# A dense weight loaded in two halves, and a new order of the pieces, in a kernel of memory-augmented attention beside a SiLU layer

## The chip, the cores and the metric

The kernel runs on one core of one Trainium2 chip. The metric is the device time of one execution in microseconds, as a median of several runs. The core has five engines that work beside each other, each through its own list of instructions in order: TensorE (PE in the profile, with its weight loads as PEld), VectorE (DVE), ScalarE (ACT), GpSimd (POOL) and SyncE (SP), which here only issues transfers. ScalarE issues a few transfers too.

## What is computed

`x` is normalised by rows (layer norm), and the result is fed to two branches whose outputs are added to `x`: an attention of 32 heads of 16 columns over 2048 tokens, cut into four segments of 512 with a memory carried from segment to segment, and a dense layer pair with SiLU. Cut to what matters:

```python
def _A_ref(x, wq, wk, wv, wo, beta):          # x: 1 x 2048 x 512, H = 32, Dh = 16, N = 4 segments of L = 512
    ...
    for s in range(N):
        logits = jnp.einsum('bhqd,bhkd->bhqk', qs, ks) * scale + mask      # causal inside a segment
        a_dot = jnp.einsum('bhqk,bhkd->bhqd', _softmax(logits, axis=-1), vs)
        num = jnp.einsum('bhld,bhde->bhle', phi(qs), M)
        den = jnp.einsum('bhld,bhd->bhl', phi(qs), z)[..., None] + 1e-06
        outs.append(g * (num / den) + (1.0 - g) * a_dot)
        M = M + jnp.einsum('bhld,bhle->bhde', phi(ks), vs)
        z = z + jnp.einsum('bhld->bhd', phi(ks))
    ...
    return o @ wo

def _B_ref(x, w1, w2):                        # w1: 512 x 1792, w2: 1792 x 512
    return _silu(x @ w1) @ w2

xn = _layernorm(x)
return x + _A_ref(xn, A_wq, A_wk, A_wv, A_wo, A_beta) + _B_ref(xn, B_w1, B_w2)
```

`phi(t)` is `t + 1` above zero and `exp(t)` below.

## The kernel before, in words

All work is cut into some 1,100 pieces, each a short function, and the string `ORDER` at the top lists them by name. A loop at the end of the kernel walks the string, looks each name up in `PIECES` and calls it; nothing is rescheduled afterwards. So the order in the string is the order of the instructions on each engine, and an engine whose next instruction waits holds up all that it has behind it. Waits are on counters: one for each compute engine, and eight that the transfers of SyncE and ScalarE use in turn, so that a transfer may also wait for the one that used its counter before.

A name is letters and numbers with dots. In the list that follows `s` is the segment, `dt` a block of 128 columns (eight heads), `ft` one of 14 blocks of 128 of the 1792 dense columns, `j` one of four blocks of 128 tokens, `t` one of 16 such blocks in all.

- `xs t`, `xq`/`xi t`, `xg t.n`: row statistics on VectorE, and the reciprocal root, on ScalarE and VectorE for the first four blocks and on GpSimd (lines 275 and 278) for four blocks at once after that. `Nv t` normalises on VectorE (line 293). `X`/`Xv`/`Xa` transpose on TensorE and copy; `XD t` transposes by a transfer on SyncE (line 726) into `xnT`.
- `k`, `q` `s.dt.part`, `h s.ft.part`: half of a projection, four products of 256 columns in segment 0 (line 325) and two of 512 after it (line 314). `v s.j.part`: two of 512. `kv`, `qv`, `vv` copy out on VectorE, `ka`, `qa`, `va` on ScalarE (lines 340, 350, 357); with every copy of k GpSimd makes a second one, `kTo`, that keeps odd heads only (line 341).
- `S t`: one of 80 score batches, `t = 20 s + 5 dt + b`. TensorE fills the one score tile `psS` (four of the eight banks, line 642), ScalarE takes the exponential of 128 x 2048 scores (line 649), GpSimd clears the masked corner in one or two instructions (line 657). Batches with `b` of 0 and 3 have one instruction of 512 columns, 2 one of 1024, 1 and 4 two of 512.
- `E n`, `O n`: products of the weights with v for even and odd heads (line 676), each of five batches' exponentials. `Ev`/`Ea`, `Ov`/`Oa` copy out (lines 699 and 706) and move rows by transfers on SyncE: two for an even copy, six for an odd one (lines 691 and 710).
- `ha s.ft`, `hv s.ft`: SiLU, a tanh on ScalarE (line 438) and a product on VectorE (line 443). `fp`/`gp`, `fa`/`ga`, `fv`/`gv`: phi of k and of q on GpSimd, ScalarE and VectorE (lines 368, 374, 384). `tanh` is one small operation on beta.
- `t`, `m`, `mv`, `mw`: the memory's update. `s`, `sv`, `r`, `w` (and `R`, `W` in the last segment): denominators and their reciprocals. `d`/`dv` and `z`/`zv`: two transfers each that spread them over rows (line 523, four buffers) and a product on VectorE (lines 545, 535). `n`/`nv`: the memory's part of the output (lines 549, 556).
- `o s.j.i`: one product of the output, `i` below 14 with `w2`, above with `wo` (line 595). `oh i.half` is half of such a product for the last block of tokens. `xl s.j` loads a block of x again (line 562), `st s.j` and `sh half` add it and store (lines 569, 574; 613, 617).
- `lw i`: a load of a weight on ScalarE's queue (line 176). The other weights are loaded from SyncE at the very start.

`psS` is one tile, so a score batch waits for the exponential before it. All other results on TensorE share four banks, each taken again when the copy that empties it is done.

The lines that the prediction follows most are these:

```python
psS = psatt.tile([P, 4, L], F32, name="psS")          # psatt has one buffer
exp = nc.scalar.activation(out=Pb[:, :, :], in_=psS[:, :, :], func=AF.Exp, scale=SCALE)
...
def load_w(eng, w_sb, W, k0, k1):
    eng.dma_start(out=w_sb[:, k0:k1, :], in_=W.rearrange("(ko ki) n -> ki ko n", ki=P)[:, k0:k1, :])
```

Of the kernel before, what the change touches and what calls it, by code (L numbers as in the profile page):

```python
# [16 lines left out]
ones0 ones1 zeros xs0 xs1 xq0 xi0 busy44 xq1 Nv0 xi1 X0.1 Nv1 Xa0.1 busy6 X1.1 Xa1.1 v0.0.0 xs2 xs3 xq2 v0.0.1 xq3 xi2 va0.0 v0.1.0 Nv2 v0.1.1 va0.1 xi3 X2.1 Nv3 odd tb Xv2.1 k0.0.0 X3.1 Xv3.1 q0.0.0 q0.0.1 qv0.0 k0.0.1 xs7 xs4 ka0.0 k0.2.0 xs6 fp0.0  # L17
S0 v0.3.0 k0.1.0 k0.2.1 fa0.0 xs5 xg4.4 v0.3.1 kv0.2
S2 q0.1.0 k0.1.1 q0.1.1 vv0.3 fp0.2 v0.2.0 kv0.1 fa0.2 Nv7 Nv4
S1 qv0.1 v0.2.1 h0.10.0 h0.10.1 h0.7.0 xs8 vv0.2 ha0.10 h0.7.1 hv0.10 ha0.7  # L20
S4 Nv5 h0.4.0 h0.4.1 ha0.4 h0.11.0 hv0.7 k0.3.0 h0.11.1 ha0.11 xs9 hv0.11 fv0.2
S7 k0.3.1 q0.3.0 XD4 q0.3.1 hv0.4 q0.2.0 XD5 XD7 q0.2.1 fa0.1
S6 qv0.3 qv0.2 h0.13.0 h0.13.1 t0.2 v1.3.0 ha0.13 v1.1.0
S3 v1.1.1 kv0.3 Nv6 xs11 h0.5.0 hv0.13 h0.5.1 xs10 ha0.5 xg8.4 XD6 E0 vv1.1
S5 v1.3.1 lw0 hv0.5 vv1.3 k1.0.0 xs14 k1.2.0 k1.2.1
S9 h0.1.0 Ev0 Nv10 kv1.2 Nv9 h0.1.1 k1.0.1 E1 ha0.1
S13 kv1.0 h1.11.0 XD10 h0.2.0 h0.2.1 ha0.2 h1.11.1 Ev1 fv0.0 hv0.1
S8 hv0.2 tanh O0 h0.8.0 h0.8.1 bmask Ov0 q1.1.0 ha0.8 hv0.8
# [12 lines left out]
S20 r0.3 h1.10.1 k2.1.0 o0.0.3 ha1.10 hv1.0 k2.1.1 r0.1 q2.3.0
S23 r0.2 o0.0.7 gate kv2.1 q2.3.1 r0.0 xg12.4 xl0.0 h1.4.0 h1.4.1 w0 o0.0.13 hv1.10 qv2.3 ha1.4 o0.0.12
S28 z0.3 o0.1.12 o0.1.0 hv1.4 z0.0 z0.2 o0.0.4 E4 lw1 O4
S27 o0.1.11 Ev4 Ov4 k2.0.0 o0.1.2 h1.5.0 h1.5.1 o0.0.11 ha1.5 Nv12 z0.1
S25 o0.0.9 o0.0.8 o0.1.1 zv0.3 k2.0.1 hv1.5 zv0.0 fv1.2 q2.1.0 XD12 ga1.3 fp1.3 o0.0.1 kv2.0 o0.0.5
S29 o0.1.8 o0.1.6 fa1.3 o0.0.14 q2.1.1 h1.1.0 zv0.2 o0.1.9 o0.1.17 qv2.1
S26 o0.2.0 o0.0.17 h1.1.1 o0.1.14 o0.1.7 fv1.3 xl0.1 o0.2.7 gp1.3 zv0.1 ha1.1 t1.0 hv1.1 o0.1.16 o0.1.13
S30 o0.0.15 o0.0.16 st0.0 o0.1.15 o0.2.14 t1.3 ga1.1 o0.2.8 o0.1.10 E5 Nv14
S31 gv1.3 o0.2.1 Ev5 h1.3.0 fp1.1 fa1.1 o0.2.4 o0.1.4 o0.2.3 Nv15 O5 mw0.0
S32 o0.1.3 XD14 o0.1.5 h1.3.1 o0.2.10 o0.2.17 o0.2.9 o0.2.12 mw0.2 xl0.3 ha1.3 st0.1 o0.2.6  # L50
S33 Ov5 o0.2.16 o0.2.5 t1.2 o0.2.11 fv1.1 ga1.0 k2.3.0 v2.0.0 Nv13 gp1.0 hv1.3 k2.3.1
S38 v2.0.1 o0.2.15 kv2.3 h1.6.0 h1.6.1 o0.2.2 ha1.6 XD15 vv2.0 o0.2.13
S34 gv1.0 o0.3.3 hv1.6 h1.13.0 h1.13.1 v2.3.0 st0.2 q2.2.0 ha1.13
S37 ga1.2 t1.1 q2.2.1 o0.3.16 o0.3.6 gp1.2 hv1.13 o0.3.2 qv2.2 o0.3.5 E6
S36 v2.3.1 Ev6 o0.3.7 vv2.3 h1.12.0 o0.3.1 gv1.1 h1.12.1 ha1.12 o0.3.12
S35 hv1.12 fa2.0 fp2.1 XD13 O6 q2.0.0 q2.0.1 gv1.2 h1.2.0
S39 Ov6 q3.3.0 xl1.1 q3.3.1 h1.2.1 qv2.0 E7 ha1.2 qv3.3 Ev7
S40 k3.1.0 hv1.2 k3.1.1 o0.3.0 o0.3.9 O7 ga2.2 Ov7 kv3.1
S47 fp2.0 o0.3.4 m1.2 q3.1.0 q3.1.1 mv1.2 qv3.1 s1 sv1
S41 r1.0 m1.0 v3.3.0 o0.3.11 o0.3.8 xl1.0 fv2.0 mv1.0 v3.3.1 va3.3 o0.3.17 r1.3 fp2.2  # L60
S44 o0.3.15 h2.3.0 q3.0.0 fa2.1 q3.0.1 v3.1.0
S42 r1.2 r1.1 v3.1.1 qv3.0 h2.3.1 o0.3.13 w1 o0.3.14 d1.1 z1.1 vv3.1 o0.3.10 ha2.3 fv2.1 v3.0.0 hv2.3
S43 t2.0 st0.3 v3.0.1 h2.4.0 h2.4.1 z1.2 E8 vv3.0 ha2.4
S45 hv2.4 h1.7.0 h1.7.1 dv1.1 k3.2.0 k3.2.1 o1.0.0 fa2.2 o1.0.5 ha1.7
# [37 lines left out]
def kernel(  # L102
# [13 lines left out]
    nc = tc.nc  # L116
# [4 lines left out]
    DT = D // P  # L121
# [7 lines left out]
    FT = F // P  # L129
# [28 lines left out]
    w2_sb = cpool.tile([P, FT, D], BF16, name="w2_sb")  # L158
# [16 lines left out]
    def load_w(eng, w_sb, W, k0, k1):  # L175
        eng.dma_start(out=w_sb[:, k0:k1, :], in_=W.rearrange("(ko ki) n -> ki ko n", ki=P)[:, k0:k1, :])  # L176
# [618 lines left out]
```

## Time and profile before

| | us |
|---|---|
| median of three runs | 231.92 (231.20 to 232.23) |
| the profiled execution, its whole time | 231.23 |
| its span in the profile | 229.50 |
| TensorE busy with products | 221.5 (97%) |
| ScalarE busy | 198.9 (87%) |
| VectorE busy | 171.8 (75%) |
| GpSimd busy | 114.8 (50%) |
| 80 exponentials, line 649 | 150.2, 1.88 each |
| first and last exponential start | 12.86 and 206.06 |

The granted clock of TensorE is full in every slice of the span. Products are pipelined: the mean of one that the profile lists (0.38 us for 512 columns) is longer than the distance at which they follow each other (0.216 us), so a busy TensorE is not yet one at its peak. In a timeline row the columns are start and duration in microseconds, engine, line, operation, output and inputs, shapes and count; in brackets stands the idle time of the engine before it, with what ended it. In the chain of waits the run is followed back from its end, at each step to what released it.

Where the time of the middle goes, by stretches of the span (all us):

| stretch | TensorE | VectorE | ScalarE | GpSimd |
|---|---|---|---|---|
| 0 to 10 | 8.17 | 6.08 | 5.40 | 3.49 |
| 20 to 30 | 9.87 | 9.14 | 9.99 | 5.33 |
| 90 to 100 | 10.00 | 7.32 | 9.96 | 6.25 |
| 180 to 200 | 19.98 | 16.01 | 18.56 | 9.02 |
| 215 to 229.5 | 11.00 | 7.98 | 0.00 | 0.00 |

### The profile page before, as it was taken

The page shows a single profiled execution, that of the slowest core. Times are in us where ns is not written, and L with a number is a line of the kernel's source. Part 1 is how long each engine was busy: PE and PEld are TensorE (multiplying, and loading weights), DVE is VectorE, ACT ScalarE, POOL GpSimd, SP SyncE. Part 2 cuts the span into 40 slices and gives each one's busy share as a digit, 9 for nine tenths or more (in the row PEclk, how much of TensorE's full clock was granted, in tenths as well). Part 3 has the DMA queues.
Part 4 walks back from the last instruction along what each step waited for, and adds up shares of the span by engine and source line. Part 5 has one row for each costly group of instructions (what it writes and reads, how often), then busy time and mean ns, then how long its engine had stood idle before and what let it go on. Part 6 is the DMA issues. An engine that isn't in the chain of part 4 may idle for free.

```text
span 229.5 us, 5243 instructions
## 1 busy us (share of the span) xinstructions
PE 221.5 (97%) x1984; PEld 103.6 (45%) x1984; DVE 171.8 (75%) x349; ACT 198.9 (87%) x179; POOL 114.8 (50%) x173
## 2 busy tenths in 40 slices
PE   7899999989999999999999999999999999999993
PEld 7657645445533433333433433344433443434552
DVE  4699997978978758866596967845796868874744
ACT  3789999999999999999999999999999999996000
POOL 6068557576474586564574474655444473332000
PEclk9999999999999999999999999999999999999999
DMA  6993256014302424241115232203032111132132
GB/s 200 366 371 70 57 169 195 18 31 74 73 17 54 140 72 101 59 94 30 33 38 98 75 83 76 64 9 98 25 96 81 52 32 58 32 88 83 34 116 94
DMA packets 34778, 20.40 MB, mean 89 GB/s; under 512 B 15680, under 2 KB 34240, under 8 KB 34752
## 3 DMA queue, kind: packets, MB, share of 16 engines
q1 hardware_dynamic: 32128, 17.45, 27.6%
q10 hardware_dynamic: 2624, 2.62, 3.7%
q8 instruction: 15, 0.25, 0.5%
q14 instruction: 11, 0.09, 0.1%
HBM read 9.96 MB, written 2.10 MB: 53 GB/s over the span
## 4 chain that ended last, share of the span: by engine, by line
PE 77%; ACT 13%; DMA 3%; issue 2%; DVE 1%; SPq 1%; DVEq 0%; ACTq 0%
PE ps L314 26%; PE psO L595 25%; PE psS L642 10%; ACT Pb L649 10%; PE psV L676 8%; DMA wq_sb<-in_A_wq_dram 3%; PE psS L595 3%; PE ps L325 3%; ACT th L438 2%; PE ps L549 1%; ACT ex L374 1%; PE psM L400 1%; SPq L176 1%; DVE hT L443 1%; DVE o_out L569 1%
## 5 line engine op out<-in xcount | busy, mean ns | idle before, releaser
L649 ACT ACTIVATE Pb<-psS 128x2048 bf16<-128x2048 f32 x80 | 150.2, 1878 | 5.2 <-PE psS L642 4.0
L657 POOL TENSOR_SCALAR_AFFINE_SELECT Pb<-Pb 128x512 bf16<-128x512 bf16 (+1 forms) x112 | 81.2, 739 | 82.2 <-ACT Pb L649 81.8
L595 PE MATMUL psO<-w_sb,hT 128*128 128x512 bf16 x196 | 60.2, 381 | 0.0
L443 DVE SCALAR_TENSOR_TENSOR hT<-th,ps 128x512 bf16<-128x512 bf16 x56 | 37.8, 681 | 21.1 <-ACT th L438 20.9
L314 PE MATMUL ps<-xnT,w_sb 128*128 128x512 bf16 x168 | 45.5, 380 | 0.0
L595 PEld LDWEIGHTS <-hT 128*128 128x128 bf16 x238 | 22.0, 98 | 26.7 <-issue 6.6
L438 ACT ACTIVATE th<-ps 128x512 bf16<-128x512 f32 x56 | 32.6, 595 | 0.4 <-PE ps L314 0.4
L314 PEld LDWEIGHTS <-w_sb 128*128 128x128 bf16 x168 | 15.2, 98 | 18.0 <-issue 3.1
L676 PE MATMUL psV<-Pb,Vz 128*32 128x128 bf16 (+3 forms) x512 | 22.2, 301 | 0.0
L642 PE MATMUL psS<-qT,kT 16*128 16x256 bf16 (+3 forms) x256 | 17.3, 301 | 1.3 <-ACT Pb L649 0.3
L595 PE MATMUL psO<-wo_sb,oT 128*128 128x512 bf16 x56 | 18.2, 380 | 0.0
L314 PE MATMUL ps<-wv_sb,xnT 128*128 128x512 bf16 x64 | 18.0, 381 | 0.1
L642 PE MATMUL psS<-qT,kTo 32*128 32x384 bf16 (+3 forms) x256 | 17.2, 299 | 0.8 <-ACT Pb L649 0.2
L676 PEld LDWEIGHTS <-Vz 128*32 128x32 bf16 x512 | 11.0, 96 | 13.4 <-issue 5.5
L341 POOL TENSOR_SCALAR kTo<-kT,pm_odd 128x512 bf16<-128x512 bf16 x16 | 11.9, 745 | 10.2 <-ACT kT L340 8.2
L325 PE MATMUL ps<-xnT,w_sb 128*128 128x256 bf16 x112 | 14.6, 273 | 0.0
L706 DVE CAST odd<-psV 128x512 bf16<-128x512 f32 x15 | 10.3, 686 | 4.9 <-PE psV L676 4.8
L314 PE MATMUL ps<-xnT,wk_sb 128*128 128x512 bf16 x48 | 13.3, 380 | 0.1
L350 DVE CAST qT<-ps 128x512 bf16<-128x512 f32 x16 | 10.8, 680 | 3.5 <-PE ps L314 2.2
L642 PEld LDWEIGHTS <-kT 16*128 16x128 bf16 x256 | 5.8, 91 | 16.7 <-issue 15.5
L314 PE MATMUL ps<-xnT,wq_sb 128*128 128x512 bf16 x48 | 12.8, 380 | 0.0
L325 PEld LDWEIGHTS <-w_sb 128*128 128x128 bf16 x112 | 10.4, 98 | 3.9 <-issue 1.5
(95 smaller groups left out, 258.0 us busy)
## 6 DMA issues: line engine op xcount, KB each, us to landing
spr<-rz SPq DMA_DIRECT2D x56, 64.0 KB
x_res<-in_A_x_dram SPq DMA_DIRECT2D x16, 128.0 KB
out_dram<-o_out SPq DMA_DIRECT2D x15, 128.0 KB
w_sb<-in_B_w_dram SPq DMA_DIRECT2D x1, 1792.0 KB
w_sb<-in_B_w_dram ACTq DMA_DIRECT2D x1, 1792.0 KB
x_hi<-in_A_x_dram SPq DMA_DIRECT2D x2, 512.0 KB
oraw<-odd SPq DMA_DIRECT2D x64, 16.0 KB
wv_sb<-in_A_wv_dram SPq DMA_DIRECT2D x2, 256.0 KB
```

The lines of the kernel that those rows point to most:

```text
L314: nc.tensor.matmul(sts[s][key][:, :], lhsT=lhsT(ki), rhs=rhs(ki), start=(ki == 0), stop=(ki == DT - 1))
L325: nc.tensor.matmul(sts[s][name, i][:, cols], lhsT=w_sb[:, ki, i * P : (i + 1) * P], rhs=xnT[:, ki, cols], start=(ki == 0), stop=(ki == DT ...
L341: nc.gpsimd.tensor_scalar(out=kTo[:, dt, :], in0=kT[:, dt, :], scalar1=pm_odd[:, 0:1], scalar2=1.0, op0=ALU.mult, op1=ALU.mult,)
L350: copy(out=seg_tile(s, "qT")[:, dt, :], in_=sts[s].pop(("q", dt))[:, :])
L438: nc.scalar.activation(out=th[:], in_=sts[s]["h", ft][:, :], func=AF.Tanh, scale=0.5)
L443: nc.vector.scalar_tensor_tensor(out=st["hT"][:, ft, :], in0=st.pop(("th", ft))[:], scalar=1.0, in1=st.pop(("h", ft))[:, :], op0=ALU.add, ...
L595: mm = nc.tensor.matmul(st["psO", *key], lhsT=lhsT, rhs=rhs, start=len(done) == 1, stop=len(done) == FT + DT)
L642: nc.tensor.matmul(psS[:, g, c0 : c0 + nq], lhsT=kk[rows, dt, kt * P : (kt + 1) * P], rhs=st["qT"][rows, dt, kt * P : L], start=True, stop ...
L649: exp = nc.scalar.activation(out=Pb[:, :, :], in_=psS[:, :, :], func=AF.Exp, scale=SCALE)
L657: mask = nc.gpsimd.affine_select(out=blocks, in_=blocks, compare_op=ALU.is_ge, fill=0.0, base=0, pattern=[[0, blocks.shape[1]], [1, P]], c ...
L676: nc.tensor.matmul(psV[32 * g : 32 * g + 32, kt * P : L], lhsT=Vzs[s % 2][:, kt, 4 * dt + g, par : par + 2, :].rearrange("p a d -> p (a d) ...
L706: copy(out=odd[:], in_=sts[s].pop(("psV", 1))[:, :])
```

## The change

`w2` (14 blocks of rows) was loaded by one transfer, `lw0`, of 1792 KB behind S5; now `lw0` loads its first seven blocks behind S7 and `lw1` the other seven behind S14. `wo`, which was `lw1` behind S28, is now `lw2` behind S26. And the whole string `ORDER` is a new one: the same pieces in another order, with other choices of the engine for a few copies (`qa0.0`, `ka0.2`, `va3.2` and `Oa14` on ScalarE where they were on VectorE; `va3.3`, `ka3.0` and `Ea9` the other way). No function is changed.

The diff, cut to the start, the loads and the end. The string's last line, very long, is wrapped here:

```diff
@@ ORDER
-... Xv2.1 k0.0.0 X3.1 Xv3.1 q0.0.0 q0.0.1 qv0.0 k0.0.1 xs7 xs4 ka0.0 k0.2.0 xs6 fp0.0
-S0 v0.3.0 k0.1.0 k0.2.1 fa0.0 xs5 xg4.4 v0.3.1 kv0.2
-S2 q0.1.0 k0.1.1 q0.1.1 vv0.3 fp0.2 v0.2.0 kv0.1 fa0.2 Nv7 Nv4
-S1 qv0.1 v0.2.1 h0.10.0 h0.10.1 h0.7.0 xs8 vv0.2 ha0.10 h0.7.1 hv0.10 ha0.7
...
-S5 v1.3.1 lw0 hv0.5 vv1.3 k1.0.0 xs14 k1.2.0 k1.2.1
...
-S28 z0.3 o0.1.12 o0.1.0 hv1.4 z0.0 z0.2 o0.0.4 E4 lw1 O4
...
-S79 w3 h3.13.0 h3.13.1 ha3.13 hv3.11 o2.1.15 xl2.1 o2.1.1 h3.6.0 h3.10.0 hv3.13 d3.3 o2.1.0
-S78 o2.1.14 h3.10.1 R0.3 h3.9.0 h3.6.1 R0.1 o2.1.13 d3.0 o2.1.11 R0.0 o2.1.6 R0.2 W0 ha3.10
-S76 o2.1.9 hv3.10 ha3.6 o2.1.3 d3.1 o2.1.8 h3.9.1 o3.1.0 o3.1.2 dv3.0 o3.1.13 ha3.9 dv3.3
...
- st3.2 o3.1.10 oh13.0 o3.0.17 o3.1.15 o3.1.17 o3.1.3 sh0 oh16.1 oh9.1 st3.0 oh4.1 st3.1 oh1.1 oh15.1 oh0.1 oh17.1 oh7.1 sh1
+... Xv2.1 k0.0.0 X3.1 Xv3.1 xs4 k0.2.0 xs5 k0.0.1 q0.0.0 ka0.0 xs7 q0.0.1 k0.2.1 k0.3.0 xs6 qa0.0 xg4.4 ka0.2
+S2 q0.1.0 v0.3.0 k0.1.0 k0.3.1 kv0.3 fa0.2 fp0.2
+S3 q0.1.1 qv0.1 fa0.0 v0.3.1 Nv6 k0.1.1 h0.7.0
+S1 Nv7 v0.2.0 Nv5 v0.2.1 Nv4 XD6 h0.7.1 ha0.7 vv0.3 kv0.1 h0.11.0 vv0.2 xs10
+S4 hv0.7 XD5 xs9 XD4 h0.11.1 q0.2.0 h0.4.0 XD7 h0.4.1 ha0.11
+S8 xs11 ha0.4 v1.1.0 v1.1.1 hv0.11 q0.2.1 vv1.1 xs8 h0.13.0
+S0 qv0.2 h0.10.0 hv0.4 h0.10.1 h0.13.1 ha0.10 h0.2.0 fp0.0 ha0.13 q1.1.0 xg8.4
+S7 q1.1.1 h0.2.1 fv0.2 hv0.10 hv0.13 E0 O0 lw0
+S9 qv1.1 fp0.3 Ev0 h0.5.0 xs12 ha0.2 Nv10 v1.3.0 h0.5.1 Ov0 t0.2 v1.3.1
...
+S14 kv1.0 v1.0.1 qv0.3 q1.0.0 q1.0.1 lw1 E1 qv1.0
...
+S26 r0.0 q2.3.1 k2.0.0 lw2 hv1.10 k2.0.1 o0.0.9 qv2.3 v2.2.0
...
+S75 h3.2.0 h3.2.1 o2.2.3 hv3.8 O14 Oa14 s3 ha3.2
+S78 o2.2.5 sv3 h3.11.0 xl2.1 r3.3 h3.11.1 st2.2 r3.1 h3.7.0 o2.1.17 r3.0 h3.7.1 o2.1.3 ha3.11 hv3.2 r3.2
+S76 o2.1.2 w3 o2.1.0 o2.1.4 hv3.11 o2.1.13 h3.9.0 d3.3 ha3.7 h3.9.1 o2.1.16 ha3.9 o2.1.7 R0.3 d3.2 o2.1.14
+S79 R0.0 d3.1 R0.1 R0.2 hv3.7 o2.1.9 h3.6.0 W0 o2.1.11 h3.6.1 o2.1.10 h3.10.0 ha3.6 o2.1.12 h3.10.1 hv3.9 ha3.10 o2.1.8 hv3.6
+S77 d3.0 o3.0.12 hv3.10 o3.0.9 dv3.3 o3.0.2 h3.13.0 h3.13.1 o2.1.6 ha3.13 o2.1.15 z3.0 dv3.2 o2.1.5 hv3.13
+ oh12.0 o3.0.8 o3.2.3 oh6.0 o3.0.11 oh5.0 o3.0.0 dv3.0 o2.1.1 z3.2 st2.1 E15 O15 o3.1.3 xl3.1
...
+ oh5.1 xl3.2 oh17.1 o3.1.17 xl3.3 o3.0.17 o3.2.15 o3.2.17 o3.2.9 o3.1.8 oh11.0 oh10.0 oh13.1 o3.1.15 oh2.1 oh15.1
+ oh1.1 oh14.1 st3.0 o3.1.1 oh17.0 st3.2 sh1 o3.1.9 o3.1.12 sh0 st3.1
@@ PIECES
-        "lw": lambda i: load_w(nc.scalar, *((w2_sb, B_w2, 0, FT), (wo_sb, A_wo, 0, DT))[i]),
+        "lw": lambda i: load_w(nc.scalar, *((w2_sb, B_w2, 0, FT // 2), (w2_sb, B_w2, FT // 2, FT), (wo_sb, A_wo, 0, DT))[i]),
```

## The prediction

> **What bounds the kernel now.** I read the page first, then ScalarE's timeline between the exponentials, then the two ends of the run on all engines, and last the waits of SyncE's queue.
>
> ```profile
> PE 221.5 (97%) x1984; PEld 103.6 (45%) x1984; DVE 171.8 (75%) x349; ACT 198.9 (87%) x179; POOL 114.8 (50%) x173
> PE 77%; ACT 13%; DMA 3%; issue 2%; DVE 1%; SPq 1%; DVEq 0%; ACTq 0%
> ```
>
> TensorE looks like the limit, with ScalarE behind it. The timeline of ScalarE says how the two are tied:
>
> ```profile
> 30.27 1.88 ACT L649 ACTIVATE Pb<-psS 128x2048 bf16<-128x2048 f32 x1
> 30.28 0.39 ACTq L176 DMA_DIRECT2D w_sb<-in_B_w_dram  x1
> 32.65 1.88 ACT L649 ACTIVATE Pb<-psS 128x2048 bf16<-128x2048 f32 x1 [0.50 <-PE psS L642]
> 34.42 0.59 ACT L438 ACTIVATE th<-ps 128x512 bf16<-128x512 f32 x1
> 35.05 1.88 ACT L649 ACTIVATE Pb<-psS 128x2048 bf16<-128x2048 f32 x1
> ...
> 198.06 1.88 ACT L649 ACTIVATE Pb<-psS 128x2048 bf16<-128x2048 f32 x1 [0.18 <-PE psS L642]
> 199.84 1.08 ACT L438 ACTIVATE th<-ps 128x512 bf16<-128x512 f32 x2
> 200.79 1.90 ACT L649 ACTIVATE Pb<-psS 128x2048 bf16<-128x2048 f32 x1
> ```
>
> Exponentials start 2.38 us apart whether one small ScalarE operation stands between them (32.65 to 35.05) or none (30.27 to 32.65): there is one score tile psS, so an exponential must end, the next scores be written and the next exponential start. The beat is 2.375 us (the usual gap in this timeline). It is lengthened by two things only: two small operations in one gap (198.06 to 200.79; the six such gaps average 2.753, so +0.378 each), or more than 2.375 us of TensorE pieces between two score batches. So the run is three parts: the first exponential starts at 12.86; 79 gaps take 193.20 (last start 206.06) of which 79 x 2.375 = 187.63 is the beat and 5.57 is excess; the tail from there to the span's end at 229.50 is 23.44.
>
> **The change part by part.** The arithmetic is the same; each part is costed against these three.
>
> *The load.* One issue of 0.39 us on ScalarE's queue becomes two, and wo's issue moves. All three stand in gaps that hold no small operation (behind S7, S14, S26); the row at 30.28 shows such an issue under an exponential and the gap still 2.38. Cost 0; without that cover, 0.39 each. The two halves start at about 27.8 and 37.7 (beats counted from 12.86). w2 is first read by o0.0.7, near 64: over twenty microseconds of other work hide the second half. In the built program the second issue waits for the completion of a row move of O0, since the eight completion counters go round; that move is issued near 33, five microseconds earlier. On SyncE the sixth transfer of O0's copy waits for the first half, which has had about 7 us by then; behind it stand only t0.2 and XD10, whose readers are many beats away. Cost 0.
>
> *The start.* wq is awaited until 10.25 with TensorE idle 0.65 now; the new list puts k0.2.0 and k0.0.1 there. But S2 needs qa0.0 too and ScalarE also takes ka0.2 before the exponential. From rows: k0.0.1 ends 10.56, q0.0.1 11.43 (0.109 us a 256-wide product), qa0.0 runs 11.65 to 12.24, scores at 12.4, exponential at 12.85. Gain 0.0.
>
> *GpSimd before S8.* The rstd pair xg4.4 now stands ahead of kT's odd copy ka0.2, of S2's mask and of everything up to kv0.1, whose odd copy the fifth batch S8 reads.
>
> ```profile
> 12.46 0.70 POOL L341 TENSOR_SCALAR kTo<-kT,pm_odd 128x512 bf16<-128x512 bf16 x1 [8.18 <-ACT kT L340]
> ...
> 15.81 1.03 POOL L278 TENSOR_TENSOR rstd_all<-rstd_all,expo 128x4 f32<-128x4 f32 x1
> ...
> 16.92 1.03 DVE L293 TENSOR_SCALAR xn_t<-x_hi,mv_all,rstd_all 128x512 bf16<-128x512 bf16 x2
> 16.94 0.86 POOL L341 TENSOR_SCALAR kTo<-kT,pm_odd 128x512 bf16<-128x512 bf16 x1
> ```
>
> xg4.4 waits for four row statistics, which start when x's second load has landed: after wq's 10.25 in the same queue and before 11.95, where the first one ran without waiting for it. Taking 11.75 and the 3.28 us the four took, they end at 15.03, xg4.4 at 16.34 (0.20 + 1.03 and a gap). Then 0.86 (odd copy), 1.12 (mask), 0.70, 0.63, 0.64, 1.23, 0.70 from the GpSimd groups: 22.2, while S8 could be written at 12.86 + 3 x 2.375 + 1.88 + 0.06 = 21.9. Cost 0.3. Bounds: 0 if the data lands at 10.25; 1.5 if three odd copies take the longest of the trace (1.01), with the longest mask (1.42) and pos (0.78).
>
> The row to see is the last: beside two normalisations the odd copy took 0.86 instead of 0.70, and they 1.03 instead of 2 x 0.41. The Trainium skill (GPSIMD Engine Reference, Specifications) says that GpSimd shares its SBUF interface with VectorE, contending when VectorE runs in a 2-port mode or has two SBUF inputs; Trainium Architecture — The Big Picture (What this means for kernel authors) calls it an exclusive lock. The trace agrees that both stretch. It speaks against this change, for all four normalisations now fall beside the GpSimd chain; a full lock of 4 x 0.41 us would be an estimated 1.6 instead of the 0.16 taken here.
>
> *The gaps.* Gaps with two small operations go from six to nine (S0, S5, S11, S62, S66, S60, S75, S76, S79), gaps with none from four to seven, which gives nothing back. Eight at 0.378 are 3.02. In the ninth, S79, TensorE is longer still: four halves of h (8 products), five o, at 0.216 each (four L314 products in 0.86 in the chain of waits), 0.21 for the scores and 2 x 0.10 for the changes of tile shape: 3.22, excess 0.84. S71 and S74 have 2.57 and 2.47: 0.29. In S75, ScalarE's first operation is the copy Oa14, which waits for O14: 0.15. With S8's 0.3 that is 4.60. The same bookkeeping gives 3.85 for before, whose gaps show 5.57: 1.72 is small waits it does not name (S18, S30, S44, S61, S75 and dust). I charge the new list the same 1.72; nothing in VectorE's or SyncE's work per gap says otherwise. Bounds 0.5 and 3.0. Excess 6.32, or 0.75 more; the last exponential starts at 206.81.
>
> *The tail on TensorE.* Behind the last scores stand 66 products of 512 columns instead of 67, and 36 of 256 in both: -0.2. Now the last product is issued at 225.73 and ends 225.84, 19.78 after the last exponential; that becomes 19.57: 226.38.
>
> *The last stores.*
>
> ```profile
> 223.98 0.69 DVE L569 SCALAR_TENSOR_TENSOR o_out<-psS,x_res 128x512 bf16<-128x512 f32 x1 [1.79 <-PE psS L595]
> 224.59 0.41 DVE L613 SCALAR_TENSOR_TENSOR o_half<-psS,x_res 128x256 bf16<-128x256 f32 x1
> 224.92 1.28 DVE L569 SCALAR_TENSOR_TENSOR o_out<-psO,x_res 128x512 bf16<-128x512 f32 x2
> 226.11 0.41 DVE L613 SCALAR_TENSOR_TENSOR o_half<-psS,x_res 128x256 bf16<-128x256 f32 x1
> ```
>
> Now st3.2 starts 0.31 after oh17.0 is issued, and 2.2 us of products remain to cover it. In the new list oh17.0 stands third from the end, 0.54 before TensorE finishes, and st3.2, sh1, sh0, st3.1 queue behind it on VectorE: 0.31 + 0.61 + 0.33 + 0.33 + 0.68 after its issue, by the row distances above. So the last store is issued at 226.38 - 0.54 + 2.26 + 0.05 = 228.15 against 227.06, and the span ends 2.44 later as now: 230.6.
>
> **Sum.** +0.75 - 0.21 + 0.55 = +1.1 on 229.50. What lies around the span is 231.23 - 229.50 = 1.73, so 232.3 beside the profiled 231.23. That execution is 0.69 under the median 231.92; on the median's scale I forecast **233.0**, 0.47% longer, at the edge of the 0.5% that a measurement of this kernel can tell from no change.
>
> **The rivals.**
>
> *GpSimd decides (slower).* If its chain before S8 takes the upper price, the beat slips 1.5 instead of 0.3: 234.2. It decides once kv0.1's odd copy ends after 21.9. For: 0.86 and 1.01 among the copies. Against: thirteen of the sixteen copies took 0.69 to 0.71.
>
> *SyncE's tail (slower).* E15 to nv3.3 runs through row moves, reciprocals and a spread: E15 starts 209.39 and nv3.3 ends 222.19 now, 12.8 us. In the new list E15 starts near 210.3, and oh17.1, the first reader, is due 3.14 us before TensorE ends, at 223.24: a margin of 0.1 to 0.2 after the same 12.8. st2.1 and xl3.1 now stand ahead of the moves (0.4), two x_res loads no longer ahead of the spread (0.45). Beyond that each microsecond counts in full; one more, like the spread waits of 2.3 and 1.1 in VectorE's list, gives 233.9.
>
> *The waits go (faster).* If the 1.72 of unnamed waits came from late SyncE transfers and the new list avoids them, and nothing else changes: 231.3; with the final stores overlapping as now, 230.7. For: in S18 the reader k2.2.0 follows two transposes (XD8, XD11) by one beat; in the new list only XD9 stands so near its reader. Against: SyncE's longest waits are for VectorE, not the reverse.
>
> *The split load holds ScalarE.* If O0's row move completes after 39, the second issue holds every exponential behind it; two microseconds late is 235. The margin above is some four.
>
> **How the numbers follow.** Forecast 0.48 (own range 232.0 to 234.0), GpSimd 0.16, SyncE's tail 0.18, waits go 0.14, held ScalarE 0.04. Slower by over 0.5% (above 233.08): all of three rivals, 0.38, less a little that is made up elsewhere, and a fifth of the forecast: 0.46. Faster (below 230.76): 0.10 of the waits' 0.14 and a little of the forecast's low end: 0.12. The rest 0.42. The range leaves a tenth out at each side: 230.9 to 234.7.
>
> **What would show it.** First exponential within 0.2 of 12.86; the fifth at 22.6 or 22.7 and not 24; nine gaps near 2.75 and that of S79 near 3.2; last exponential near 206.8; four stores on VectorE in a row at the end, the last a 512-wide one. The prediction is wrong if any gap before S62 exceeds 3 us, or if TensorE stands idle after the last scores.

## The result and the profile after

The changed kernel takes 233.31 us (median of 9 runs, 232.43 to 234.15), beside 232.05 us (230.85 to 233.07) for the kernel before on the same chip. The ratio is 1.0062, with a 95% interval of 1.0035 to 1.0090. Run once more in the study, beside 17 runs of before, it gave 1.0076 (1.0050 to 1.0102). By the ratios it is slower by 1.4 to 1.8 us. The profiled execution took 232.94 us, its span is 231.2 us, and the granted clock is 0.997.

The totals of the page first: busy time of each engine, and the chain that ended last by engine.

```profile
PE 221.9 (96%) x1984; PEld 102.8 (44%) x1984; DVE 172.7 (75%) x348; ACT 199.2 (86%) x180; POOL 114.0 (49%) x173
...
PE 75%; ACT 7%; DVE 6%; DMA 4%; issue 2%; SPq 2%; POOL 1%; DVEq 0%; ACTq 0%
```

The work is that of before. What changed is the chain: VectorE has 6% of it instead of 1%. So some waits on VectorE are now in the path. To find them, I split each trace at the exponentials. "Excess" is what a stretch of gaps takes beyond 2.375 us for each gap. The columns are two traces of each kernel; the second of each comes from the study.

| us | before | before, again | after | after, again |
|---|---|---|---|---|
| first exponential starts | 12.86 | 12.89 | 12.72 | 13.11 |
| excess of the first 18 gaps | 0.85 | 0.95 | 2.21 | 3.36 |
| excess of the next 43 | 1.46 | 1.57 | 0.25 | 0.26 |
| excess of the last 18 | 3.27 | 3.24 | 3.59 | 3.59 |
| last exponential to the end of the span | 23.46 | 23.58 | 24.81 | 24.30 |
| span | 229.52 | 229.85 | 231.22 | 232.25 |

The new order loses 1.3 to 2.5 us in the first 18 gaps, gains 1.2 to 1.3 in the middle, loses 0.3 in the last gaps and 0.7 to 1.4 in the tail. About 0.4 us of the first two figures is only a shift: the kernel before has two gaps with two small operations among its first 18 and one in the middle (S45, 2.77 us), the new list has three and none. Here are the places, all from the timeline of after. First the gaps of ScalarE with a load issue, and with two small operations:

```profile
28.08 0.39 ACTq L176 DMA_DIRECT2D w_sb<-in_B_w_dram  x1
28.18 1.90 ACT L649 ACTIVATE Pb<-psS 128x2048 bf16<-128x2048 f32 x1
30.58 1.88 ACT L649 ACTIVATE Pb<-psS 128x2048 bf16<-128x2048 f32 x1 [0.50 <-PE psS L642]
...
200.35 1.88 ACT L649 ACTIVATE Pb<-psS 128x2048 bf16<-128x2048 f32 x1
202.12 1.08 ACT L438 ACTIVATE th<-ps 128x512 bf16<-128x512 f32 x2
203.16 1.88 ACT L649 ACTIVATE Pb<-psS 128x2048 bf16<-128x2048 f32 x1
```

These behave as forecast: 2.40 us over the load's issue, 2.81 with two operations. The same timeline, at the start:

```profile
16.23 2.83 DVE L293 TENSOR_SCALAR xn_t<-x_hi,mv_all,rstd_all 128x512 bf16<-128x512 bf16 x4
16.28 0.83 POOL L341 TENSOR_SCALAR kTo<-kT,pm_odd 128x512 bf16<-128x512 bf16 x1
...
17.07 1.14 POOL L657 TENSOR_SCALAR_AFFINE_SELECT Pb<-Pb 128x1024 bf16<-128x1024 bf16 x1
...
18.98 0.67 DVE L357 CAST Vz<-ps 128x512 bf16<-128x512 f32 x1
...
19.71 0.60 PE L325 MATMUL ps<-xnT,w_sb 128*128 128x256 bf16 x4 [0.71 <-DVE Vz L357]
...
20.69 1.88 ACT L649 ACTIVATE Pb<-psS 128x2048 bf16<-128x2048 f32 x1 [0.68 <-PE psS L642]
```

Four normalisations stand in a row on VectorE and take 2.83 us, where the four of the first blocks took 0.41 each. The copy vv0.3 behind them ends at 19.65. The product h0.11.0 needs the bank that this copy empties, and S4's scores stand behind h0.11.0 on TensorE. So the exponential of S4 starts 3.04 us after that of S1. And at the end of the span:

```profile
226.03 0.69 DVE L569 SCALAR_TENSOR_TENSOR o_out<-psS,x_res 128x512 bf16<-128x512 f32 x1 [1.48 <-PE psS L595]
226.63 0.75 DVE L613 SCALAR_TENSOR_TENSOR o_half<-psS,x_res 128x256 bf16<-128x256 f32 x2
227.19 1.13 SPq L617 DMA_DIRECT2D out_dram<-o_half  x2
227.30 0.68 DVE L569 SCALAR_TENSOR_TENSOR o_out<-psO,x_res 128x512 bf16<-128x512 f32 x1
228.43 0.38 SPq L574 DMA_DIRECT2D out_dram<-o_out  x1
```

VectorE stood idle for 1.48 us before the first of four pieces that then follow each other without a gap, and the last store is issued at 228.43, 22.03 us after the last exponential (21.00 before). It is a whole block of 128 KB, and the span ends 2.79 us later; before, it was a half of 64 KB and 2.46 us. TensorE is not what differs: its last product starts 19.64 us after the last exponential, 19.67 before. From that product to the issue of the last store it is now 2.38 us instead of 1.33.

The second trace of after shows one more place. These are SyncE's transfers in it (start, and how long the issue held the queue), and then the wait view of the same queue (microseconds waited in total, times, longest):

```profile
38.72 1.27 SPq L726 DMA_TRANSPOSE xnT<-xn_t  x1
...
43.36 2.21 SPq L726 DMA_TRANSPOSE xnT<-xn_t  x1
46.64 0.37 SPq L562 DMA_DIRECT2D x_res<-in_A_x_dram  x1
...
54.74 2.10 SPq L726 DMA_TRANSPOSE xnT<-xn_t  x1
```

```profile
SPq L562 <- DMA xnT<-xn_t: 1.0, 1, 1.0
```

The transposition of tile 10 (38.72) is followed within 0.15 us by the load of w2's second half on ScalarE's queue (38.87). In the trace's landing records, the transposition lands between 46.14 and 46.57 and the half at 46.41. The load of a residual, xl0.1 (46.64), is the first user of the buffer that tile 10 held. It waits 1.0 us, with SyncE's queue behind it, after the issue at 43.36 had already held the queue for 2.21 us where most of line 726 hold it for 1.2 to 1.3. The queue is then busy without a break until the transposition of tile 9 at 54.74. The next rows are what waits for that:

```profile
58.24 0.59 PE L314 MATMUL ps<-xnT,wk_sb 128*128 128x512 bf16 x2 [0.91 <-DMA xnT<-xn_t]
...
59.22 1.88 ACT L649 ACTIVATE Pb<-psS 128x2048 bf16<-128x2048 f32 x1 [0.88 <-PE psS L642]
```

That is k2.1.0 in S15's place, and the gap behind S15 is 3.24 us. In the first trace SyncE came to xl0.1 only at 45.20, when tile 10 had landed, and xl0.1 did not wait; the gap was 2.47, 0.1 over the beat.

### The profile page after: what moved, and what is told of

Its sections match the earlier page's. It is cut to its first block, busy times and chain, and to the rows that moved or that the text cites. A ratio compares the mean times of both kernels' runs of the same rounds, so it can differ in the third digit from the quotient of the medians.

```text
span 231.2 us, 5219 instructions
## 1 busy us (share of the span) xinstructions
PE 221.9 (96%) x1984; PEld 102.8 (44%) x1984; DVE 172.7 (75%) x348; ACT 199.2 (86%) x180; POOL 114.0 (49%) x173
## 3 DMA queue, kind: packets, MB, share of 16 engines
q10 hardware_dynamic: 2640, 2.62, 3.5%
## 4 chain that ended last, share of the span: by engine, by line
PE 75%; ACT 7%; DVE 6%; DMA 4%; issue 2%; SPq 2%; POOL 1%; DVEq 0%; ACTq 0%
PE ps L314 27%; PE psO L595 23%; PE psS L642 10%; PE psV L676 8%; ACT Pb L649 6%; DMA x_hi<-in_A_x_dram 3%; PE ps L325 3%; PE psS L595 3%; DVE stats L270 2%; ACT th L438 1%; DVE xn_t L293 1%; PE ps L549 1%; SPq L523 1%; SPq L176 1%; DVE hT L443 1%
## 5 line engine op out<-in xcount | busy, mean ns | idle before, releaser
L657 POOL TENSOR_SCALAR_AFFINE_SELECT Pb<-Pb 128x512 bf16<-128x512 bf16 (+1 forms) x112 | 80.2, 730 | 82.6 <-ACT Pb L649 81.6
L595 PE MATMUL psO<-w_sb,hT 128*128 128x512 bf16 x196 | 62.8, 381 | 0.0
L314 PE MATMUL ps<-xnT,w_sb 128*128 128x512 bf16 x168 | 46.4, 380 | 0.0
L676 PE MATMUL psV<-Pb,Vz 128*32 128x384 bf16 (+3 forms) x512 | 22.4, 301 | 0.0
L595 PE MATMUL psO<-wo_sb,oT 128*128 128x512 bf16 x56 | 19.3, 380 | 0.3 <-DVE oT L556 0.3
L642 PE MATMUL psS<-qT,kT 16*128 16x384 bf16 (+3 forms) x256 | 17.3, 301 | 0.7 <-ACT Pb L649 0.2
L325 PE MATMUL ps<-xnT,w_sb 128*128 128x256 bf16 x112 | 15.2, 273 | 1.0 <-DVE Vz L357 0.7
L706 DVE CAST odd<-psV 128x512 bf16<-128x512 f32 x14 | 9.6, 688 | 4.7 <-PE psV L676 4.5
L350 DVE CAST qT<-ps 128x512 bf16<-128x512 f32 x15 | 10.3, 685 | 3.4 <-PE ps L314 3.1
```

The costliest lines, as they stand in the source:

```text
L314: nc.tensor.matmul(sts[s][key][:, :], lhsT=lhsT(ki), rhs=rhs(ki), start=(ki == 0), stop=(ki == DT - 1))
L325: nc.tensor.matmul(sts[s][name, i][:, cols], lhsT=w_sb[:, ki, i * P : (i + 1) * P], rhs=xnT[:, ki, cols], start=(ki == 0), stop=(ki == DT ...
L350: copy(out=seg_tile(s, "qT")[:, dt, :], in_=sts[s].pop(("q", dt))[:, :])
L595: mm = nc.tensor.matmul(st["psO", *key], lhsT=lhsT, rhs=rhs, start=len(done) == 1, stop=len(done) == FT + DT)
L642: nc.tensor.matmul(psS[:, g, c0 : c0 + nq], lhsT=kk[rows, dt, kt * P : (kt + 1) * P], rhs=st["qT"][rows, dt, kt * P : L], start=True, stop ...
L657: mask = nc.gpsimd.affine_select(out=blocks, in_=blocks, compare_op=ALU.is_ge, fill=0.0, base=0, pattern=[[0, blocks.shape[1]], [1, P]], c ...
```

## The experiments

Each experiment but the last is the changed kernel with one or more edits. Times are medians beside runs of before on the same chip; the changed kernel again, **a0_after**, was 233.63 us.

> The changed kernel unaltered, beside the kernel before and the three edits on one chip. Theory: the two kernels differ by the end of the span (last store issued 1.37 us later, landing 0.33 us longer) and by 0.34 us in the last exponential, so the ratio is 1.006 to 1.008 again. Rival (the difference is one chip's or one day's): a ratio within 0.998 to 1.002.

Ratio 1.0076 (1.0050 to 1.0102): the difference holds. Here the two kernels differ by less at the end than in the first pair (0.7 us instead of 1.4) and by more at the start (2.4 instead of 1.4).

**e1_start: the normalisations spread.**

```diff
-S3 q0.1.1 qv0.1 fa0.0 v0.3.1 Nv6 k0.1.1 h0.7.0
-S1 Nv7 v0.2.0 Nv5 v0.2.1 Nv4 XD6 h0.7.1 ha0.7 vv0.3 kv0.1 h0.11.0 vv0.2 xs10
-S4 hv0.7 XD5 xs9 XD4 h0.11.1 q0.2.0 h0.4.0 XD7 h0.4.1 ha0.11
+S3 q0.1.1 qv0.1 fa0.0 v0.3.1 vv0.3 Nv5 k0.1.1 h0.7.0
+S1 kv0.1 v0.2.0 v0.2.1 XD5 h0.7.1 ha0.7 vv0.2 h0.11.0 Nv6
+S4 hv0.7 XD6 Nv4 h0.11.1 q0.2.0 h0.4.0 XD4 Nv7 XD7 h0.4.1 ha0.11
...
```

> VectorE's first normalisations of segment 1 are spread, one behind each copy, instead of four in a row, and two statistics go later. Theory: the four in a row (2.83 us beside GpSimd's work) held back the copy that frees the bank of h0.11, so the gap of 3.04 us before the exponential of S4 and that of 2.55 us before S1 fall to about 2.40, and the time falls by 0.6 to 0.85 us against the changed kernel. Rival (GpSimd's chain in front of S8's scores): the scores of S4 or S8 then wait for the odd copy, the fifth exponential stays at 23.0, and the time stays. Second rival (the work on VectorE is only moved): the stall comes back within the next three gaps, time within 0.2 us.

234.07 us, ratio 1.0106 (1.0074 to 1.0138): no gain, perhaps a loss. Both gaps that the theory named fell to 2.375 us, so the cause of the stall was right. But 0.39, 0.39 and 0.35 us came back behind S4, S7 and S9: VectorE is short of time there. The second rival was right that the work is only moved, though the time rose by 0.4 us, more than its 0.2. Besides, this execution had a stall in the middle that neither trace of after had:

```profile
121.82 6.33 SPq L523 DMA_DIRECT2D spr<-rz  x8
...
127.98 0.46 DVE L535 TENSOR_TENSOR oT<-spr,oraw 128x512 bf16<-128x512 bf16 x1 [1.46 <-DMA spr<-rz]
...
129.09 1.02 PE L314 MATMUL ps<-xnT,wk_sb 128*128 128x512 bf16 x4 [0.63 <-DVE oraw L699]
...
131.14 1.88 ACT L649 ACTIVATE Pb<-psS 128x2048 bf16<-128x2048 f32 x1 [1.29 <-PE psS L642]
```

The same eight spreads in a0_after:

```profile
122.10 5.25 SPq L523 DMA_DIRECT2D spr<-rz  x8
```

One of the eight issues held SyncE for 1.68 us instead of 0.60. zv1.1 waited for its tile, the copy Ev8 behind it on VectorE was late, and k3.2.0 waited for the bank. This cost 1.3 us in two gaps.

**e2_end: another order of the last products and stores.**

```diff
-... o3.2.9 o3.1.8 oh11.0 oh10.0 oh13.1 o3.1.15 oh2.1 oh15.1 oh1.1 oh14.1 st3.0 o3.1.1 oh17.0 st3.2 sh1 o3.1.9 o3.1.12 sh0 st3.1
+... o3.2.9 st3.0 o3.1.8 o3.1.15 st3.2 o3.1.1 o3.1.9 o3.1.12 st3.1 oh11.0 oh10.0 oh17.0 sh0 oh13.1 oh2.1 oh15.1 oh1.1 oh14.1 sh1
```

> The products after the last scores are put in another order so that the four last pieces of output end one after another, the last two as halves: the stores stand on VectorE before the last half's products are issued. Theory (the end of the span is the queue of four stores): the last store is issued at about 227.1 instead of 228.4, lands 2.4 us later instead of 2.8, and the time falls by 1.0 to 1.7 us. Rival (the last products or SyncE's chain in front of them set the end): the last store follows TensorE's end, which does not move, and the time falls by less than 0.4 us.

232.63 us, 1.0 less than a0_after, at the low end of what was expected; ratio 1.0040 (1.0018 to 1.0061).

```profile
226.72 2.06 SPq L574 DMA_DIRECT2D out_dram<-o_out  x3
227.72 0.69 DVE L569 SCALAR_TENSOR_TENSOR o_out<-psO,x_res 128x512 bf16<-128x512 f32 x1 [0.39 <-PE psO L595]
228.33 0.75 DVE L613 SCALAR_TENSOR_TENSOR o_half<-psS,x_res 128x256 bf16<-128x256 f32 x2
229.20 0.81 SPq L617 DMA_DIRECT2D out_dram<-o_half  x2
```

The last exponential of this trace starts at 208.56 (the first one started late, at 14.14), so the end of the span at 232.24 is 23.68 behind it. Over all traces the distance from the last exponential to the end is 24.26 to 24.85 in seven traces with the changed kernel's end (mean 24.48), and 23.14 to 24.00 in five with this one (mean 23.54); before has 23.46 and 23.58. So the end of the order costs 0.9 to 1.0 us. Where it goes can be read from the start of TensorE's last product to the issue of the last store: 2.38 to 2.41 us in all seven, 1.35 in four of the five (0.91 in e10, which issues one store on ScalarE), 1.33 and 1.52 in the two of before. The queue of four pieces behind the last products is the cause. The size of the last store is not shown to be one: from its issue to the end of the span the seven take 2.60 to 2.86 us with a block of 128 KB, the five 2.53 to 3.07 with a half of 64 KB.

**e4_gaps: the loads issued from SyncE, small operations into the freed gaps.**

```diff
-S0 qv0.2 ... ha0.10 h0.2.0 fp0.0 ha0.13 q1.1.0 xg8.4
-S7 q1.1.1 h0.2.1 ...
+S0 qv0.2 ... ha0.10 h0.2.0 fp0.0 q1.1.0 xg8.4
+S7 ha0.13 q1.1.1 h0.2.1 ...
...
-        "lw": lambda i: load_w(nc.scalar, ...
+        "lw": lambda i: load_w(nc.sync, ...
```

> The three weight loads are issued from SyncE's queue at the same places, and of the small ScalarE operations, one of S0's two goes to S7, one of S5's two to S6 and S6's one to S14. Theory: a second small operation in a gap costs 0.38 us and a load issue takes ScalarE's gap without lengthening it, so two gaps of 2.73 to 2.77 become 2.38 and S7 and S14 stay at 2.38: the last exponential 0.75 us earlier, the time 0.6 to 0.8 us less. Rival (the small operations only wait where they stand, and the loads' issues on SyncE hold back its moves): under 0.2 us, or slower.

235.95 us, 2.3 us more: a clear miss. The gaps of S0 and S5 did shrink (to 2.62 and 2.37), but those behind S7 and S6 became 4.25 and 4.11:

```profile
31.54 0.73 PE L676 MATMUL psV<-Pb,Vz 128*32 128x512 bf16 x16 [1.56 <-DVE hT L443]
...
32.65 1.88 ACT L649 ACTIVATE Pb<-psS 128x2048 bf16<-128x2048 f32 x1 [1.88 <-PE psS L642]
```

The tanh that was moved past one exponential delays its SiLU on VectorE by a beat, the SiLU empties a bank, and O0 on TensorE wants that bank. Behind S6 it is the same: a product of v waits 1.35 us for the SiLU of the second moved tanh. A second operation in a gap costs 0.38 us; to move it to the next gap costs five times that where the four banks have no spare.

**e3_one_load: w2 in one piece at the first half's place.**

```diff
-        "lw": lambda i: load_w(nc.scalar, *((w2_sb, B_w2, 0, FT // 2), ...
+        "lw": lambda i: load_w(nc.scalar, *((w2_sb, B_w2, 0, FT), ...
-S14 kv1.0 v1.0.1 qv0.3 q1.0.0 q1.0.1 lw1 E1 qv1.0
+S14 kv1.0 v1.0.1 qv0.3 q1.0.0 q1.0.1 E1 qv1.0
```

> The changed kernel with w2 loaded in one piece at S7 (the first half's place); the second half's place in S14 stays empty. Theory (the second half's transfer holds up SyncE): the transposition of tile 10, issued 0.1 us before that load, landed 7.4 us later, at 46.1 to 46.6; the load of the residual (xl0.1) waits 1.0 us for its buffer, with SyncE's queue behind it, so the transposition of tile 9 is issued at 54.7 and the product of S15 waits 0.9 us for it. Without that load tile 10 lands within 3 us, xl0.1 does not wait, the gap of S15 falls from 3.24 to about 2.40, and the time falls by 0.6 to 0.9 us against the changed kernel. Rival (the split costs nothing, as forecast): S15's gap and the time stay within 0.3 us. Second rival (the one long transfer of about 11 us holds the moves of the first heads' sums instead): a stall before S14, time up by 0.5 us or more.

235.36 us, 1.7 us more than a0_after: the theory's forecast was wrong, the second rival right in direction, though not in the place (the gaps up to S14 were hardly longer). Tile 10's transposition landed 2.4 us after its issue, so the second half's load had indeed held it. But now the row moves of the first heads (31.06 to 33.42) landed only at 36.0 to 37.5, with the load, and SyncE waited for them:

```profile
SPq L710 <- DMA zraw<-oraw: 3.3, 1, 3.3
```

The queue was later than in a0_after (tile 9's transposition at 55.10) and the gap behind S15 3.40. In this order, one piece is worse than two by the times. The trace does not show all of it: it is of the fastest of the six executions (234.30), and its first 18 gaps have only 0.2 us more than a0_after's. In the kernel before, one piece (issued 30.28, landed by 37.99) held the row moves of E0 in the same way (issued from 33.11, landed by 38.29), but the moves of the odd heads, which come after them, were issued only at 39.07, and nobody waited. No run has the split load in the old order.

**e7_xl_late: xl0.1 behind tile 9's transposition.**

```diff
-S13 Nv9 h1.11.0 vv1.0 k1.1.0 k1.1.1 xl0.1 hv0.1 ...
+S13 Nv9 h1.11.0 vv1.0 k1.1.0 k1.1.1 hv0.1 ...
-S19 v1.2.1 hv0.9 ha0.6 kind XD9 O2 E2 vv1.2 Ev2 hv0.6
+S19 v1.2.1 hv0.9 ha0.6 kind XD9 xl0.1 O2 E2 vv1.2 Ev2 hv0.6
```

> The changed kernel with one word moved: the residual's load xl0.1 is issued on SyncE behind the transposition of tile 9 (S19) instead of ahead of that of tile 11 (S13). Both halves of w2 stay. Theory (xl0.1 waits on SyncE for the buffer that tile 10's late transposition holds): the transposition of tile 9 is issued about 1.0 us earlier, the gap of S15 is 2.40 to 2.50 in place of 3.24, and the time falls by 0.6 to 0.9 us. Rival (SyncE is late for other reasons, its moves and transpositions of the keys alone): S15's gap stays above 3.0 and the time within 0.2 us.

S15's stall is gone (excess of the first 18 gaps 2.45 instead of 3.36), but the time is 233.57, ratio 1.0095 (1.0058 to 1.0132): no less. Its trace had the slow spread of e1_start (1.56 us), with gaps of 3.17 and 2.90 behind S47 and S50.

Two more things stand in the runs. The stall follows the landing of tile 9. In all twelve traces of the new order, where that landing comes up to 1.21 us after the start of S15's exponential, the gap is 2.38 to 2.41; at 1.36 it is 2.47, and at 2.07 to 2.34 it is 3.18 to 3.40. With xl0.1 moved the landing comes at 0.81 to 1.19 in five of five traces. And the time of a whole execution is not the span alone. What lies around the span is 1.7 to 1.85 us in a0_after, in before and in most other runs, but 2.0 to 2.15 in every execution of e1, e3, e7 and e11. Why is open. By the median span e7 is at 231.5 us, 0.4 under a0_after.

**e11_xl_zv: in addition, zv1.1 behind the copy Ev8**, so that a late spread holds nobody:

```diff
-S46 ... zv1.1 d1.2 Ev8 d1.0 ...
+S46 ... d1.2 Ev8 zv1.1 d1.0 ...
```

> The run with xl0.1 issued behind the transposition of tile 9, and on VectorE the product zv1.1 moved behind the copy Ev8 (one word). Theory: moving xl0.1 did end S15's stall of 0.85 us, and what it gave was taken by another thin wait: zv1.1 waited 1.3 to 1.5 us for its spread tile, with the copy Ev8 and TensorE's k3.2.0 behind it, and the gaps of S47 and S50 were 3.17 and 2.90. With Ev8 ahead these two stay under 2.65, and the time is 0.6 to 1.2 us under the changed kernel's 233.6. Rival (the time lost is elsewhere, in transfers that vary from one execution to the next): no gain, 233.3 to 233.8.

233.20 us, ratio 1.0081 (1.0049 to 1.0113): 0.4 us less than a0_after by the medians, nothing by the ratios (the median span, 231.1 us, is 0.8 less). In its trace the slow spread fell elsewhere (near 211), so the edit was not put to the test. What S15's wait costs in most executions is not shown by this pair.

**Together.** e8 is e2's end with e7's word; e9 adds the edit at the start below; e12 is e9 with xl0.1 back in S13; e10 is e9 with zv1.1 behind Ev8, a statistic behind the silu of h0.11, and the first half's store on ScalarE's queue.

```diff
-S1 Nv7 v0.2.0 Nv5 v0.2.1 Nv4 XD6 h0.7.1 ha0.7 vv0.3 kv0.1 h0.11.0 vv0.2 xs10
-S4 hv0.7 XD5 ...
+S1 Nv7 v0.2.0 vv0.3 Nv5 v0.2.1 Nv4 XD6 h0.7.1 ha0.7 kv0.1 h0.11.0 vv0.2
+S4 hv0.7 xs10 XD5 ...
```

> The move of xl0.1 and the new end of the order together. Theory (the two costs are separate): the gains add up, 1.0 us of the new end and 0.6 to 0.9 us of xl0.1, so 231.7 to 232.1 us beside 233.6 of the changed kernel, level with the kernel before. Rival (they cover one another, or the second is not there): 232.4 to 232.8 us.

> As the run before, and on VectorE the copy vv0.3 goes ahead of two of the four normalisations and one statistic (xs10) behind the silu of h0.7. Theory (the four in a row hold back the bank of h0.11): the gap before S4's exponential falls from 3.0 to 3.6 to 2.4 and little comes back later, so 0.4 to 0.9 us less than the run before and faster than the kernel before. Rival (VectorE is short of time there, so that its lateness only moves): the stall appears in S8's or S0's gap, and the time stays within 0.2 us.

> The run of 231.4 us (new end, vv0.3 ahead of two normalisations, xl0.1 late) with xl0.1 back in its place in S13; it differs from the changed kernel by the two ends of the order alone. Theory (the two ends are the whole difference to the kernel before; SyncE's lateness at xl0.1 costs nothing that the times can tell): 231.2 to 231.8 us, level with the kernel before. Rival (S15's wait of 0.85 us for tile 9 is paid in most executions): S15's gap is 3.2 again, and the time 232.0 to 232.4 us.

> All that helped, together: xl0.1 behind tile 9's transposition, zv1.1 behind Ev8, vv0.3 ahead of two normalisations, the new end of the order; besides, one statistic (xs11) behind the silu of h0.11, and the first half's store issued from ScalarE's queue instead of SyncE's. Theory (each is a cost of its own): beside the run without the last three (231.4 us), 0.2 us less in the gap of S8, 0.4 us less at the end, and up to 0.4 us of zv1.1's stall: 230.4 to 230.9 us, and faster than the kernel before by 0.7 to 1.2 us. Rival (the chain to the last scores has other thin waits): within 0.3 us of 231.4.

| | median us | ratio to before (95%) | median span, us (beside before's) |
|---|---|---|---|
| a0_after | 233.63 | 1.0076 (1.0050 to 1.0102) | 231.9 (+1.8) |
| e2: end | 232.63 | 1.0040 (1.0018 to 1.0061) | 230.8 (+0.7) |
| e8: end, xl0.1 | 232.03 | 1.0038 (1.0010 to 1.0067) | 230.3 (+0.4) |
| e12: end, start | 232.53 | 1.0032 (1.0009 to 1.0054) | 230.75 (+0.35) |
| e9: end, xl0.1, start | 231.42 | 0.9987 (0.9961 to 1.0012) | 229.65 (-0.25) |
| e10: all and three more | 231.57 | 0.9988 (0.9965 to 1.0010) | 229.85 (-0.05) |

e9 is level with the kernel before, not faster as forecast, and e10 is no better and misses its 230.4 to 230.9. e8's median lies in its forecast, but its ratio is that of e2. e12 fits neither side: its time is above both ranges, and the rival's stall at S15 is not in its trace. In e9's timeline vv0.3 is ready in time, and S4's exponential follows S1's by 2.375 us:

```profile
16.31 1.66 DVE L293 TENSOR_SCALAR xn_t<-x_hi,mv_all,rstd_all 128x512 bf16<-128x512 bf16 x2
...
17.89 0.68 DVE L357 CAST Vz<-ps 128x512 bf16<-128x512 f32 x1
17.94 1.88 ACT L649 ACTIVATE Pb<-psS 128x2048 bf16<-128x2048 f32 x1 [0.37 <-PE psS L642]
...
18.49 1.02 DVE L293 TENSOR_SCALAR xn_t<-x_hi,mv_all,rstd_all 128x512 bf16<-128x512 bf16 x2
...
20.31 1.88 ACT L649 ACTIVATE Pb<-psS 128x2048 bf16<-128x2048 f32 x1
```

Part of the stall came back: 0.25 us behind S8, and 0.39 in front of S1 (the gap behind S3 is 2.77, and 2.96 in e12, 3.11 in e10; it is 2.375 in a0_after and 2.67 in e8). The first 18 gaps have an excess of 1.89 us, 0.3 less than in e8. By the ratios, the start edit is worth 0.5% beside e8, and xl0.1 0.45% beside e12, while each of the two added alone to e2 gave nearly nothing (0.02 and 0.08%). All of these intervals touch or overlap. By the median spans xl0.1 gives 0.2, 0.3 and 0.6 us (from a0_after to e7, from e2 to e8, from e12 to e9), but the kernel before, run as a case of its own (b0_before), comes out 0.25 beside itself. That both are needed together would fit a chain of transfers that sets a time at S15: TensorE freed of the first stall runs into the second. In e12's trace xl0.1 does wait 1.3 us, but tile 9 lands 1.21 us after the start of S15's exponential, just in time, and there is no stall; so this is argued and not shown.

**b0_before: the kernel before, with a second trace.**

> The kernel before unaltered, with a profile of its own. Theory (the changed kernel's own list has the waits on transfers): again no gap over 2.65 us among the first 62 exponentials other than those with two small ScalarE operations, and the last exponential 193.0 to 193.6 us behind the first, while the changed kernel's two traces have 193.7 and 194.8. Rival (the first trace of before was a lucky one and the kernel varies as much): a gap of 3 us or more there, and 194 us or more.

Ratio 1.0000 (0.9974 to 1.0026). The last exponential starts 193.38 us behind the first, as expected; one gap with a single operation was 2.73, a little over the bound. The first trace of before was no lucky one.

## Why the prediction was right, and where it was not

The forecast was 233.0 us, on the median's scale, and 233.31 was measured (+0.47% forecast, +0.62% measured, interval from 0.35). The direction and the size were right, the way there only in part: four terms were wrong, three too small and one too large, and that the sum came so near is partly luck. The forecast's excess of all gaps was 6.32 us and the first trace has 6.05, but with other parts; the second has 7.21.

- **The gaps of ScalarE: right.** Of the nine gaps with two small operations eight had 2.73 to 2.81 us and that of S79 3.24 (forecast 3.22); S71 and S74 2.59 each, and the gaps over a load's issue 2.38 to 2.40. The last 18 gaps lost 0.33 us.
- **The unnamed small waits: too large.** "I charge the new list the same 1.72" failed. Take from the 6.05 of excess in the first trace the named gaps (4.58) and the stall around S1 (0.85): about 0.6 are left, 1.1 less than charged. The 43 gaps of the middle have 0.25 instead of 1.46 to 1.57, and 0.4 of that difference is the gap of S45. So the rival that the waits go was right for about two thirds of its 1.72. Which waits went, and why, no run tests.
- **The start: the wrong engine.** "GpSimd before S8", 0.3, took the shared time as 0.16 and put the lateness on GpSimd's chain. VectorE paid: the four normalisations took 2.83 and 3.20 us in the two traces of after instead of 4 x 0.41, which is 1.19 and 1.56 more, and of this 0.85 (with the gap behind S3) and 1.22 reached the exponentials. The full lock that the prediction named beside its sum, 1.6, was the better price. The sign by which it was to be called wrong, a gap of over 3 us before S62, did appear. S8's exponential came at 23.06, not at 22.6 or 22.7. "It is lengthened by two things only" is where the step is missing: TensorE also waits inside a gap, here for a bank that VectorE empties late.
- **The load: not free.** "Cost 0" was right for ScalarE and for w2's reader, and wrong for the transfers under way beside it. The prediction did look at XD10 behind a load, and stopped at "whose readers are many beats away". That holds for tile 10's reader, but not for the next user of its source buffer, xl0.1, and SyncE's whole queue stands behind that. Price in the traces: a stall of about 0.85 us behind S15 in three of the five traces with two halves and xl0.1 in S13 (a0_after, e1, e2; 0.1 in the first of after, none in e12), and in none of the five where it was moved (e7 to e11). xl0.1's own wait is not all of SyncE's delay: it is 1.0, 0.2 and 1.7 us in these three, and where it is 0.2 the issue in front of it held the queue for 3.1. In the times the price is open: 0.2 to 0.6 us by the median spans, within what repeats differ by.
- **The last stores: right in kind, too small.** The four pieces queue on VectorE as forecast, and the last is a whole block. The distance from the last exponential to the end was forecast as 23.8; seven traces have 24.48 on average. VectorE's queue was priced well: its last piece ends 1.93 us after the start of TensorE's last product in after, by the forecast's sum 1.83. What was put too small is what follows: SyncE, still busy with two halves (1.13 us for both issues), issues the last store 0.45 us after that and not 0.05, and the span ends 2.60 to 2.86 us later and not 2.44.
- **SyncE's tail: not in the form named, but not nothing.** The chain from E15 on held up nobody. But in the first trace a spread's issue at 209.78 held SyncE for 1.69 us instead of 0.60, and TensorE stood idle for 0.30 us on oT at 214.77; "or if TensorE stands idle after the last scores" was the other sign of being wrong. In the second trace, where the slow issue took 0.97, TensorE did not wait, and its last product starts 0.48 us sooner after the last exponential. This is what the tails of the two traces (24.81 and 24.30) differ by.
- **Held ScalarE: no.** Both issues of w2 took 0.39 us.

So the change is slower because it spends more than twice what it saves in the middle (1.2 to 1.3 us): about 1.0 us at the end, shown by e2, 0.3 in the last 18 gaps, and 1.3 to 2.5 before S17. Of the start's part the cause of the stall is shown by e1's and e9's timelines, where it goes from S4; what it costs in time is shown only together with xl0.1, and there the intervals still touch.

## What to carry to other kernels

When a large transfer is moved, list what else is in flight beside it, and for each the next user of its *source* buffer as well as of its result: a ring buffer passes the delay to a queue that has nothing to do with the load. Look at the last stores as a queue of their own: end with the smallest piece, and issue the stores of the others before its products end. In a list with many thin waits, a stall that is freed early may come back a few batches later (e1, e9); here the end paid at once, and the two edits near the start showed a gain only together, which the intervals do not make certain.

## What the runs showed of the hardware

*VectorE beside GpSimd.* One view of the tile xn_t in after, from 14 to 22 us (durations are minimum, median and maximum in ns):

```profile
L293 DVE TENSOR_SCALAR xn_t<-x_hi,mv_all,rstd_all x4: 404/741/1180, 16.2 to 18.3; 128x512 bf16<-128x512 bf16 x4
```

The same instruction takes 0.41 alone and 1.18 us where GpSimd's mask of 1.14 us runs beside it. The copies out of PSUM beside GpSimd's next masks kept their 0.67. The Trainium skill (Trainium Architecture — The Big Picture, What this means for kernel authors) calls the port pair that VectorE and GpSimd share an exclusive lock and not a split of bandwidth. The trace agrees for the normalisation: of the eight in the two traces of after, seven ran beside a GpSimd instruction that had begun before them or with them, and each of the seven ended 0.14 to 0.15 us after that instruction did.

*Small transfers beside a large load.* The first records of a transposition of 128 KB landed 7.4 us after its issue beside a load of 896 KB from the other queue (a0_after), and 2.4 us after without it (e3). Row moves of 2 KB had landed in full 4.1 to 5.3 us after theirs beside a load of 1792 KB (e3), and 1.6 us after in a quiet stretch of before (50.72).

*A slow issue.* In 12 of 12 traces of the new order one of SyncE's 56 spreads held the queue for 1.0 to 1.7 us instead of 0.60, three times near 125 us and nine times between 209 and 213; in neither trace of before did one. Near 125 it cost 0.2 to 1.3 us in the gaps of S47 and S50. Behind the last scores, in the four traces where it took 1.66 us or more (after, e2, e11, e12), TensorE waited 0.28 to 0.34 us for oT and its last product started 19.61 to 19.78 us after the last exponential; in the other eight it is 19.16 to 19.56. Its cause is open.
